# A gate row moved to the second issuing queue, x tiles copied in halves, two groups of loads planned earlier and a new scheduler seed, in a kernel for gated attention and feed-forward

## The chip, the cores and the metric

The kernel runs on one core of a Trainium2 chip. The metric is the time of one execution in device microseconds (us), and lower is better. An execution is timed several times; its state is "fast" where no core shows a lowered clock and the time is within 1.5% of the best of the same kernel.

The core has five engines that run their own instruction streams: PE (the tensor engine), ACT (ScalarE), DVE (VectorE), POOL (GpSimd) and SP (SyncE), which in this kernel only issues transfers. Engines wait for one another by semaphores.

## The reference, cut to what matters

```python
# x: [1, 2048, 512] bf16; 32 heads of 16; 4 segments of 512 tokens; F = 1792
g = sigmoid((x * gate_w).sum(-1, keepdims=True))
# a: per segment, masked softmax attention plus a read of a memory M, z
for s in range(4):
    a_dot = softmax(q_s @ k_s.T * 0.25 + mask) @ v_s
    a_mem = (phi(q_s) @ M) / (phi(q_s) @ z + 1e-6)     # phi(t) = t + 1 if t > 0 else exp(t)
    o_s = sigmoid(beta) * a_mem + (1 - sigmoid(beta)) * a_dot
    M, z = M + phi(k_s).T @ v_s, z + phi(k_s).sum()
a = concat(o) @ wo
b = (relu(x @ W_gate) * (x @ W_up)) @ W_down
out = g * a + (1 - g) * b
```

`gate_w` is one row of 512 values (1 KB). All 2048 tokens are multiplied by it, so the kernel keeps it copied to all 128 partitions, in `gwb`.

## The kernel before: the parts that the change and the argument touch

The program is not written in its final order. A list scheduler in it is given operations, each with what it reads and writes, a priority and, for some, an earliest planned time (`after`, in ns of a plan). A seeded random jitter breaks near-ties. The result is a fixed program for each engine. So an edit of a planned time or of the seed can change the order of everything.

```python
sc = Sched(seed=197)
...
def load(eng, names, dst, src, nbytes, occ=460.0):          # one transfer, on ACT's or SP's ring
    (lact if eng == "act" else lsp).append(dma(eng, lambda e, ...: e.dma_start(dst, src), ...))
x0 = A_x[0, 0:512, :].rearrange("(i p) d -> p i d", p=128)
for n, src in enumerate((A_wq[0:16, 0:32], gate_w[0:32].partition_broadcast(16),
                         W_g[0:16, 0:32], W_u[0:16, 0:32], W_d[0:16, 0:32])):
    load("act", [f"touch{n}"], V.touch[0:16, n, :], src, 1024)   # 1 KB reads whose data nobody uses
for i in range(4):
    load("sp", [f"hT{i}"], V.hT[:, i, :], x0[:, i, :], 1 << 17)  # the four x tiles of segment 0
for nm, w, src in (("wq", V.wq, A_wq), ("wk", V.wk, A_wk), ("wv", V.wv, A_wv)):
    for kt in range(KT):
        if nm == "wk" and kt == 0:
            load("sp", ["gwb"], V.gwb[:], gate_w.partition_broadcast(128), 1 << 17)
        load("sp", [f"{nm}{kt}"], w[:, kt, :], src[kt * 128:(kt + 1) * 128, :], 1 << 17)
... # then beta, W_gate and W_up in eight pieces each half, x of segment 1, wo, and at last:
load("sp", ["wd"], V.wd[:], W_d.rearrange("(f p) n -> p f n", p=128), NF * 128 * 1024)
...
for c in range(2, NSEG):                                    # x of segments 2 and 3 ("chunks")
    load_x(c)                                               # four transposing transfers
    for t in lsp[-KT:]:
        t.after = 30000.0 + 10000.0 * (c - 2)
sc.queue(3, lsp)
```

Segment 0 of x comes as plain tiles `hT`, which PE transposes by a product with the identity; DVE and ACT copy the result from the accumulation banks (`psL`) to `xT`. The first q projection needs `xT`. Around these stand matmuls on constants (`warm`) that keep PE busy.

```python
xps, xcs = [warm(5, 512, 0, 3)], []
for n, (i, k0, k1, bank, eng) in enumerate(((0, 0, 4, 0, "dve"), (1, 0, 4, 1, "act"),
        (2, 0, 4, 2, "dve"), (3, 0, 2, 3, "dve"), (3, 2, 4, 0, "act"))):
    ...                                                     # PE: transpose; then the copy:
    if eng == "dve": ... e.tensor_copy(d, s_)
    else:            ... e.activation(d, s_, ACT.Copy)
xps.append(warm(5, 128, 1, 1))
```

Five names recur. `ek` and its transposed copy `phik` are phi(k) of a segment, which PE needs to update the memory. `gscr` is a 2 KB scratch in DRAM through which the gate values `gexp` are turned round to `gexpT`. `vsh` is a shifted copy of v. `osb` receives the x tiles of later segments for the gate. `wd` is the 1792 KB of W_down.

The softmax here doesn't subtract the row's maximum and nothing guards it: scores larger than these inputs give would overflow.

## Time and profile before

| | before |
|---|---|
| median of the first three runs | 272.04 us (271.92 to 272.37) |
| the run that was profiled, and its span | 272.65 us, 270.5 us |
| first q matmul, first k matmul | 5.92 us, 9.37 us |
| `wd` issued, landed | 25.78 us, 35.42 us |
| chunk 2 of x: first issue, last landing | 36.83 us, 44.60 us |
| first matmul that needs chunk 2 | 44.84 us, after a wait of 1.79 us |

All times in it but the first row are from the start of the span. The prediction shows the issue queue and PE's waits. Two more views belong beside them. The first is the head of the page's chain of waits, followed back from the last instruction: shares of the span by the engine that held up the end. The second is the table of stretches from 36 to 56 us and from 56 to 100 us: stretch, its length, then busy time and instructions of PE, of PE's weight loads, of DVE, ACT and POOL, the granted clock, the DMA share and the GB/s.

```profile
PE 87%; SPq 7%; DMA 3%; DVE 1%; issue 1%; ACT 0%
```

```profile
36.00:56.00 20.00, 17.98 (x272) 8.23 (x272) 15.00 (x29) 15.46 (x12) 9.03 (x17) 1.00 0.57 88
56.00:100.00 44.00, 43.99 (x523) 19.86 (x524) 37.55 (x74) 37.40 (x34) 22.91 (x47) 1.00 0.22 44
```

Issues and transfers hold a tenth of the chain, and PE lacks 2.02 us between 36 and 56 us and next to nothing (0.01 us) from 56 to 100 us.

### The profile page before, as it was taken

What the parts mean: (1) busy time and instruction counts of PE and PEld (TensorE: products, weight loads), DVE (VectorE), ACT (ScalarE), POOL (GpSimd) and SP (SyncE); (2) the same over time, 40 slices, a digit from 0 to 9 for tenths busy, and PEclk for the clock granted to TensorE, in tenths of its full rate; (3) what the DMA queues carried; (4) which work ended last, traced back from release to release, by engine and by line L of the source; (5) the groups of instructions that cost most, each with busy time, mean ns of one, the idle gap of its engine ahead of it and who ended that gap; (6) DMA issues with size and microseconds to landing.
All of it is one profiled execution on the core that took longest, in us unless ns stands there. A gap on an engine that the chain in (4) does not pass through costs nothing.

```text
span 270.5 us, 6903 instructions
## 1 busy us (share of the span) xinstructions
PE 264.3 (98%) x2908; PEld 117.7 (43%) x2908; DVE 187.5 (69%) x360; ACT 185.2 (68%) x160; POOL 110.4 (41%) x227
## 2 busy tenths in 40 slices
PE   7999997999999999999999999999999999999996
PEld 3344443444454435444444444444444444444444
DVE  5798786888988687787867849766666444597200
ACT  3577886787898875677787867786766567772122
POOL 5024545574248424762376225622282228220000
PEclk9999999999999999999999999999999999999999
DMA  6899994610033232210012110100111100000011
GB/s 166 233 380 197 337 130 62 101 40 22 19 63 43 61 79 61 61 21 2 21 41 61 39 41 23 41 2 0 23 41 39 41 22 19 2 0 2 0 39 41
DMA packets 35150, 17.70 MB, mean 65 GB/s; under 512 B 23984, under 2 KB 35120, under 8 KB 35120
## 3 DMA queue, kind: packets, MB, share of 16 engines
q1 hardware_dynamic: 34960, 17.26, 27.9%
q8 instruction: 23, 0.38, 0.6%
q14 instruction: 7, 0.06, 0.1%
q10 hardware_dynamic: 160, 0.01, 0.0%
HBM read 9.88 MB, written 2.11 MB: 44 GB/s over the span
## 4 chain that ended last, share of the span: by engine, by line
PE 87%; SPq 7%; DMA 3%; DVE 1%; issue 1%; ACT 0%
PE psA L879 35%; PE psA L918 18%; PE psL L747 8%; PE psA L643 7%; PE psA L911 5%; PE psA L806 5%; PE psA L641 4%; SPq L497 4%; SPq L475 2%; DMA osb<-in_A_x_dram 2%; DMA wk<-in_A_wk_dram 1%; PE psA L717 1%; PE psA L814 1%; SPq L603 1%; PE psA L688 1%
## 5 line engine op out<-in xcount | busy, mean ns | idle before, releaser
L755 ACT ACTIVATE E<-psL 128x2048 bf16<-128x2048 f32 x72 | 135.0, 1876 | 39.2 <-PE psL L747 37.6
L773 POOL TENSOR_SCALAR_AFFINE_SELECT E<-E 128x256 bf16<-128x256 bf16 x128 | 52.6, 434 | 106.9 <-ACT E L755 99.8
L879 PE MATMUL psA<-xT,wu 128*128 128x512 bf16 x224 | 59.8, 380 | 0.0
L879 PE MATMUL psA<-xT,wg 128*128 128x512 bf16 x224 | 59.4, 380 | 0.2 <-DVE hT L890 0.2
L918 PE MATMUL psA<-wd,hT 128*128 128x512 bf16 (+2 forms) x238 | 54.1, 367 | 0.0
L791 POOL TENSOR_SCALAR_AFFINE_SELECT E<-E 64x512 bf16<-64x512 bf16 (+1 forms) x64 | 41.1, 671 | 18.9 <-ACT E L755 10.7
L890 DVE TENSOR_TENSOR hT<-psA,rl 128x512 bf16<-128x512 f32 x56 | 38.0, 680 | 15.0 <-PE psA L879 13.9
L825 DVE STREAM_TRANSPOSE Tn<-psA 128x512 f32<-128x512 f32 x32 | 21.3, 696 | 18.2 <-PE psA L814 18.0
L887 ACT ACTIVATE rl<-psA 128x512 bf16<-128x512 f32 x32 | 19.1, 596 | 18.1 <-PE psA L879 17.6
L918 PEld LDWEIGHTS psA<-wd,hT 128*128 128x128 bf16 x238 | 21.3, 98 | 23.2 <-issue 1.7
L879 PEld LDWEIGHTS psA<-xT,wg 128*128 128x128 bf16 x224 | 20.4, 98 | 24.5 <-issue 1.9
L879 PEld LDWEIGHTS psA<-xT,wu 128*128 128x128 bf16 x224 | 20.2, 98 | 24.1 <-issue 2.1
L747 PE MATMUL psL<-qT,kp 32*128 32x64 bf16 (+3 forms) x768 | 28.7, 245 | 0.0
L747 PEld LDWEIGHTS psL<-qT,kp 32*128 32x128 bf16 x768 | 9.9, 92 | 30.6 <-issue 20.8
L660 DVE TENSOR_SCALAR kp<-kT,pm 128x512 bf16<-128x512 bf16 (+1 forms) x32 | 12.8, 420 | 10.6 <-PE psL L747 10.2
L888 DVE TENSOR_SCALAR rl<-psA 128x512 bf16<-128x512 f32 x24 | 16.5, 686 | 3.8 <-PE psA L879 3.2
L643 PE MATMUL psA<-xT,wq 128*128 128x512 bf16 x64 | 16.2, 380 | 2.2 <-DMA xT<-in_A_x_dram 1.8
L928 ACT ACTIVATE osb<-psA,omg 128x512 bf16<-128x512 f32 (+2 forms) x10 | 6.4, 645 | 15.7 <-PE psA L911 13.2
L806 PE MATMUL psA<-E,vaug 128*17 128x192 bf16 (+3 forms) x512 | 16.8, 273 | 0.1
L643 PE MATMUL psA<-xT,wk 128*128 128x512 bf16 x64 | 16.5, 380 | 0.4 <-DMA wk<-in_A_wk_dram 0.4
L911 PE MATMUL psA<-wo,oT 128*128 128x512 bf16 (+2 forms) x68 | 16.5, 367 | 0.0
L641 PE MATMUL psA<-wv,xT 128*128 128x512 bf16 x64 | 15.7, 380 | 0.0
(78 smaller groups left out, 235.6 us busy)
## 6 DMA issues: line engine op xcount, KB each, us to landing
out_dram<-osb SPq DMA_DIRECT2D x15, 128.0 KB, 1.7
wg<-in_B_W_gate_dram SPq DMA_DIRECT2D x8, 224.0 KB, 5.3
wu<-in_B_W_up_dram SPq DMA_DIRECT2D x8, 224.0 KB, 5.6
wd<-in_B_W_down_dram SPq DMA_DIRECT2D x1, 1792.0 KB, 9.6
osb<-in_A_x_dram SPq DMA_DIRECT2D x12, 128.0 KB, 2.1
vsh<-vaug SPq DMA_DIRECT2D x4, 136.0 KB, 2.5
hT<-in_A_x_dram SPq DMA_DIRECT2D x4, 128.0 KB, 2.4
wq<-in_A_wq_dram SPq DMA_DIRECT2D x4, 128.0 KB, 2.8
```

The lines of the kernel that those rows point to most:

```text
L641: ins = e.matmul(A(ep)[:, :], lhsT=V.xT[:, kt, tok + col * 128:tok + (col + 1) * 128], rhs=w[:, kt, :], start=(kt == 0), stop=(kt == KT - 1))
L643: ins = e.matmul(A(ep)[:, :], lhsT=w[:, kt, col * 128:(col + 1) * 128], rhs=V.xT[:, kt, tok:tok + 512], start=(kt == 0), stop=(kt == KT - 1))
L747: ins = q.matmul(PL[:, jj, o:o + w], lhsT=kap(jj), rhs=V.qT[32 * jj:32 * jj + 32, qs, q0:q0 + w], start=True, stop=True, tile_position=(32 ...
L755: acts.append(act(lambda a, eout=eout: a.activation(eout, PL[:, :, :] if slot is None else PL[:, :, :].rearrange("q h (g c) -> q h g c", g ...
L773: pools.append(pool(lambda g, ap=ap: g.affine_select(out=ap, in_=ap, compare_op=ALU.is_ge, fill=0.0, base=64, pattern=[[0, 4], [1, 64]], c ...
L791: pools.append(pool(lambda e, ap=ap, base=base: e.affine_select(out=ap, in_=ap, compare_op=ALU.is_ge, fill=0.0, base=base, pattern=[[0, 8] ...
L806: ins = q.matmul(A(eps[p])[32 * jj:32 * jj + 17, 512 - w:512], lhsT=V.vaug[:, s % 2, j, p, 4 * G + jj, :], rhs=V.E[:, e, jj, o:o + w], sta ...
L825: ds.append(dve(lambda e, p=p, ep=eps[p]: e.transpose(V.Tn[:, p, :], A(ep)[:, :]), t_dve(512), writes=[f"Tn{p}"], name=f"tr{s}_{G}_{p}", e ...
L879: ins = e.matmul(A(ep)[:, :], lhsT=w[:, kt, f * 128:(f + 1) * 128], rhs=V.xT[:, kt, c * 512:(c + 1) * 512], start=(kt == 0), stop=(kt == K ...
L890: evs.append(dve(lambda e, ep=eu, r=r, hs=hs: e.tensor_tensor(V.hT[:, hs, :], A(ep)[:, :], V.rl[:, r, :], ALU.mult), t_dve(512), reads=[f" ...
L911: ins = e.matmul(A(ep)[:, 0:c1 - c0], lhsT=V.oT[:, o0 + G, i * 128:(i + 1) * 128], rhs=V.wo[:, G, c0:c1], start=st_ and G == 0, stop=sp_ a ...
L918: ins = e.matmul(A(ep)[:, 0:c1 - c0], lhsT=V.hT[:, slots[f], i * 128:(i + 1) * 128], rhs=V.wd[:, f, c0:c1], start=st_ and f == f0, stop=sp ...
```

## The change

The intent is to take a transfer out of the crowded queue of SP, to let DVE and ACT share the copies of x more evenly, and to have chunks 2 and 3 of x earlier. The seed is new as well, and three touches are planned later. The core of the diff:

```diff
-    sc = Sched(seed=197)
+    sc = Sched(seed=140)
...
-    for n, src in enumerate((A_wq[0:16, 0:32], gate_w[0:32]..., W_g[0:16, 0:32], ...)):
+    def touch(n, src):
         load("act", [f"touch{n}"], V.touch[0:16, n, :], src, 1024)
+    touch(0, A_wq[0:16, 0:32])
+    load("act", ["gwb"], V.gwb[:], gate_w.partition_broadcast(128), 1 << 17)
...
-            if nm == "wk" and kt == 0:
-                load("sp", ["gwb"], V.gwb[:], gate_w.partition_broadcast(128), 1 << 17)
...
+    for n, w in enumerate((W_g, W_u, W_d)):
+        touch(n + 1, w[0:16, 0:32])
+        lact[-1].after = 6500.0
...
-            t.after = 30000.0 + 10000.0 * (c - 2)
+            t.after = 26000.0 + 12000.0 * (c - 2)
...
-    ... (2, 0, 4, 2, "dve"), (3, 0, 2, 3, "dve"), (3, 2, 4, 0, "act")
+    ... (2, 0, 2, 2, "dve"), (2, 2, 4, 0, "act"), (3, 0, 2, 3, "dve"), (3, 2, 4, 1, "act")
...
-                gq["dve"][-1].after = 6000.0
+                gq["dve"][-1].after = 6300.0
```

Cut from it are the names of the sixth copied piece, the pieces that the first three q projections wait for, the bank of the second `warm`, and the touch of `gate_w`, which is dropped because the gate row itself now stands in its place.

More of the change, by code (lines that the diff above doesn't have):

```diff
@@ L412, in plan @@
         ("braw", [128, 32], BF16), ("eb", [128, 32], F32), ("romgh", [128, 32], F32), ("epsv", [128, 32], F32),
-        ("gexp", [128, NT], F32), ("omg", [128, NT], F32), ("gexpT", [128, NT * 4], F32), ("c2g", [128, 2, 4, 32], F32), ("gwb", [128, 512], BF16), ("touch", [128, 5, 32], BF16), ("gl", [128, NT], F32),
+        ("gexp", [128, NT], F32), ("omg", [128, NT], F32), ("gexpT", [128, NT * 4], F32), ("c2g", [128, 2, 4, 32], F32), ("gwb", [128, 512], BF16), ("touch", [128, 4, 32], BF16), ("gl", [128, NT], F32),
         ("rden", [128, 32], F32), ("rdg", [128, 32], F32), ("rdm", [128, 128], F32), ("pm8", [128, 8], F32), ("pm", [128, 2], F32), ("pmb", [128, 64], BF16), ("ident", [128, 128], BF16),
@@ L469, in xt @@
     def xt(c):
-        return [f"xT{c}_{kt}" for kt in range(KT)] if c else [f"xT0_{i}" for i in range(5)]
+        return [f"xT{c}_{kt}" for kt in range(KT)] if c else [f"xT0_{i}" for i in range(6)]
     lact, lsp = [], []
@@ L476, in program @@
     x0 = A_x[0, 0:512, :].rearrange("(i p) d -> p i d", p=128)
-    for n, src in enumerate((A_wq[0:16, 0:32], gate_w[0:32].partition_broadcast(16), W_g[0:16, 0:32], W_u[0:16, 0:32], W_d[0:16, 0:32])):
+    def touch(n, src):
         load("act", [f"touch{n}"], V.touch[0:16, n, :], src, 1024)
+    touch(0, A_wq[0:16, 0:32])
+    load("act", ["gwb"], V.gwb[:], gate_w.partition_broadcast(128), 1 << 17)
     for i in range(4):
@@ L506, in program @@
     sc.queue(0, lsp)
+    lact = []
+    for n, w in enumerate((W_g, W_u, W_d)):
+        touch(n + 1, w[0:16, 0:32])
+        lact[-1].after = 6500.0
+    sc.queue(0, lact)
     lsp = []
@@ L549, in program @@
     xps, xcs = [warm(5, 512, 0, 3)], []
-    for n, (i, k0, k1, bank, eng) in enumerate(((0, 0, 4, 0, "dve"), (1, 0, 4, 1, "act"), (2, 0, 4, 2, "dve"), (3, 0, 2, 3, "dve"), (3, 2, 4, 0, "act"))):
+    for n, (i, k0, k1, bank, eng) in enumerate(((0, 0, 4, 0, "dve"), (1, 0, 4, 1, "act"), (2, 0, 2, 2, "dve"), (2, 2, 4, 0, "act"), (3, 0, 2, 3, "dve"), (3, 2, 4, 1, "act"))):
         def fx(e, i=i, k0=k0, k1=k1, bank=bank):
@@ L562, in program @@
             xcs.append(act(lambda e, d=dst, s_=srcp: e.activation(d, s_, ACT.Copy), t_act(w), reads=[f"bankL{bank}"], writes=[f"xT0_{n}"], name=f"xc{n}"))
-    xps.append(warm(5, 128, 1, 1))
+    xps.append(warm(5, 128, 1, 2))
     sc.queue(0, xps)
@@ L644, in fn @@
                     return ins
-                pes.append(pe(fn, mm(512, step), reads=[f"{wname}{kt}" for kt in range(k0, k0 + step)] + (xt(s) if not early or k0 > 1 else xt(s)[:4]), name=f"{name}{s}_{col}", ep=ep, role="w2" if k0 else "w"))
+                pes.append(pe(fn, mm(512, step), reads=[f"{wname}{kt}" for kt in range(k0, k0 + step)] + (xt(s) if not early or k0 > 1 else [x for x in xt(s) if x not in ("xT0_3", "xT0_5")]), name=f"{name}{s}_{col}", ep=ep, role="w2" if k0 else "w"))
             return ep
```

## The prediction

> **What bounds the kernel now.** I read the page's busy table first, then the timeline of the tensor engine (PE), the timeline of the DMA issues on SyncE (SPq), and last the timeline of VectorE (DVE) and ScalarE (ACT) in the first 13 us. First the page, then PE's timeline cut to the lines before which it stood idle.
>
> ```profile
> PE 264.3 (98%) x2908; PEld 117.7 (43%) x2908; DVE 187.5 (69%) x360; ACT 185.2 (68%) x160; POOL 110.4 (41%) x227
> ```
>
> ```profile
> 0.84 2.29 PE L545 MATMUL psL<-const-bfloat16-1.0 128*128 128x512 bf16 x5 [0.84 <-PEq L1020]
> ...
> 4.31 0.76 PE L553 MATMUL psL<-ident,hT 128*128 128x128 bf16 x8 [0.17 <-DMA hT<-in_A_x_dram]
> ...
> 5.92 3.61 PE L643 MATMUL psA<-xT,wq 128*128 128x512 bf16 x16 [0.37 <-DVE xT L560]
> ...
> 10.32 2.32 PE L643 MATMUL psA<-xT,wk 128*128 128x512 bf16 x10 [0.35 <-DMA wk<-in_A_wk_dram]
> ...
> 44.84 1.02 PE L643 MATMUL psA<-xT,wq 128*128 128x512 bf16 x4 [1.79 <-DMA xT<-in_A_x_dram]
> ...
> 55.97 0.60 PE L879 MATMUL psA<-xT,wg 128*128 128x512 bf16 x2 [0.23 <-DVE hT L890]
> ```
>
> Columns are start, length, engine and line; in brackets is the idle time ahead and what ended it. PE is the bound from about 56 us on: the table of stretches gives it 43.99 of 44.00 us from 56 to 100, and no less than 49.88 of 50 in each stretch from 100 to 250. What is left to win lies before 56 us: 0.37 before the first q projection, 0.35 for a tile of wk, 1.79 for chunk 2 of x, 0.23 behind DVE. That is 2.74 us; with the start of the x transposes nearly the whole of what any change to loads can gain, 1.0% of 272.04.
>
> The 1.79 us is the large one, and what sets it is seen in the issue queue of SyncE:
>
> ```profile
> 2.66 1.85 SPq L475 DMA_DIRECT2D wq<-in_A_wq_dram  x4
> 4.56 0.43 SPq L475 DMA_DIRECT2D gwb<-in_gate_w_dram  x1
> 5.03 1.86 SPq L475 DMA_DIRECT2D wk<-in_A_wk_dram  x4
> ...
> 25.78 0.53 SPq L475 DMA_DIRECT2D wd<-in_B_W_down_dram  x1
> 26.35 2.44 SPq L601 DMA_DIRECT2D gscr<-gexp  x1
> 28.89 7.90 SPq L667 DMA_TRANSPOSE phik<-ek  x4
> 36.83 5.17 SPq L497 DMA_TRANSPOSE xT<-in_A_x_dram  x4
> 42.10 2.90 SPq L603 DMA_DIRECT2D gexpT<-gscr  x4
> 45.04 5.03 SPq L497 DMA_TRANSPOSE xT<-in_A_x_dram  x4
> 50.11 0.58 SPq L591 DMA_DIRECT2D osb<-in_A_x_dram  x1
> ```
>
> Each row begins within 0.13 us of the end of the row above it in that timeline, from 0.80 to 50.7 us. The queue has no idle time at all, so a load comes when the queue reaches it, whatever its planned time. Chunk 2 is the last group before 42.0 us, lands at 44.6 us and PE waits until 44.84. The page's chain of waits agrees: from 34.73 to 54.65 us it runs over SPq and DMA rows, not over PE. So two bounds stand one after the other: SyncE's queue to about 55 us, then PE.
>
> Why the queue is late also shows. The 2 KB write of gscr holds the queue for 2.44 us where a plain issue takes 0.43, and the four phik transposes take 7.90 us where four xT ones take 5.17. Both stand behind wd, 1792 KB, issued at 25.78 and landed 9.6 us later by the table of DMA issues. I read this as back-pressure of the transfers ahead.
>
> **What the Trainium skill says.** "DMA: Bandwidth & Descriptors", section "Issuing engines are not separate DMA queues": DMAs from several engines run on the same 16 DMA engines and interleave; a second issuer saves only the sequencer's issue time. The trace gives that time, 0.43 us for gwb; no run yet shows the interleaving of a large load. The same page, "Queues, rings and completion order": each DMA engine takes descriptors of one ring in ring order; that fits gscr and phik landing after wd (37.2 to 39.5 against 35.4 us). "TensorE: Matmul & The Clock Gate", "Back-to-back issue gap": N/2.4 + 2.5 ns, for 512 columns 216 ns; here the first q matmuls start at 5.916 and 6.131, 215 ns apart. So PE's stream itself cannot be shortened by this change. "ScalarE: Activation LUTs", "What ACT_TABLE_LOAD costs": about 1283 ns; here one load took 1.28 us, at 3.13, right after the last of the five touch issues.
>
> **The change part by part.**
>
> Gate row. Leaves SPq: one issue of 0.43 us and its gap, 5.03 − 4.56 = 0.47 us. Everything behind it on SPq may come 0.47 us earlier. There is a second effect. Landings in the trace: the last wq at 6.79, gwb at 8.40, the first wk at 8.80, the next two 0.33 us apart. gwb's slot is thus 1.61 us, where its neighbours of equal size take about 0.33 us: some 1.28 us of transfers are delayed. On the ACT ring, issued near 1.24 us, it competes with the x tiles instead. Its 128 KB costs them at least 0.33 us; if the slow slot comes along, up to 1.3 us. wk loses it: its last tile would land about 1.3 + 0.47 us earlier than 10.18, so the 0.35 us wait goes. The gate multiplications on DVE (4 of 0.69, overlapping, about 2.5 us), which waited for gwb till 8.43 us, move into DVE's idle stretch of 2.66 us before that, and DVE reaches the q and k copies some 2 us less loaded. That is beside PE, and worth no time there by itself.
>
> Touches. ACT issued five, 0.80 to 3.10 us, then the table load until 4.42 us, and only then its copy of x tile 1 at 4.43. Now it issues two (to about 1.7 us), loads the table until about 3.0, and can copy tile 1 when PE is done with it, near 4.1: about 0.3 us earlier, beside DVE's work. The other three touches, 3 x 0.47 = 1.4 us, fall after 6.5 us, where ACT has 2.77 us idle (5.50 to 8.27). Free.
>
> Copies in halves. Before, DVE: 0.69 (tile 0), 0.69 (tile 2), 0.41 (half of 3), ending at 5.77; ACT: 0.60 and 0.38. After, DVE: 0.69 + 0.41 + 0.41, ACT: 0.60 + 0.38 + 0.38. DVE saves 0.28 us on the path to the first q matmul, 5.92 to about 5.6. Against it stands the 0.33 us or more by which gwb delays the x tiles: I book 0.0 for the start, between −0.3 and +0.5. It matters little: it is swallowed by the wait at 44.84 us, since PE cannot pass that point before chunk 2 lands.
>
> Chunks 2 and 3 forward. Planned times 30 and 40 us become 26 and 38. But the queue was full before and chunk 2 stood behind the phik transposes, which have higher priority in this program. An earlier planned time removes no wait in a full queue; it pays only if the new order puts chunk 2 ahead of phik or gexpT. The seed changes too, so the order may change. If chunk 2 went first entirely, it would gain up to four slots of 1.3 us and the wait would vanish; phik would then be later, and PE's memory update needs it (it met phik just as it landed, at 38.0 us).
>
> Sum, read at the point where PE waits for chunk 2 (44.84 us): 0.47 less issue, an estimated 0.5 less back-pressure (of the 1.28 us of delay, part is taken back by faster landings), 0.2 for the chance of a better order (about one in eight of the 1.79): −1.2 us, 270.8 us. The waits at 5.92 and 10.32 are not added, being swallowed by it.
>
> **The rivals.** (1) The order improves and the wait for x disappears. Then all the early waits count: 0.35 + 1.79 + 0.23 + about 0.3 = 2.7, so 269.4. For it speaks that the move is aimed at this wait; against it the gapless queue and phik's priority. (2) A new wait replaces the old: phik lands late and the memory update stalls, or gexpT or the first gate tile (osb landed at 54.59, DVE waited 1.16 us) gets later against a faster PE. Speaks for it that both were met with no slack; it costs 0.5 to 2 us, 271.5 to 272.8. (3) The transfer was hidden anyway: the relief on SPq is eaten behind wd, which is bound by bytes, and the gain is under 0.4: 271.7. (4) gwb's slow slot, moved to the front, delays x and wq by a microsecond: wq had 0.4 to 1.1 us of slack (wq tile 1 landed at 6.14, used at 6.56). It delays the start, mostly swallowed; at worst 272.5.
>
> **Range and chances.** I weigh the main line at half with 270.5 to 271.3, rival 1 at a quarter, the others together at a quarter. That gives 270.8 with 269.1 to 272.6 as the range. Faster by 2% needs under 266.6, 5.4 us; all waits before 56 us sum to 2.74, so only a shorter stream would do it: 3%. Slower by 2% needs 5.4 us of new waits: 2%.
>
> **What would show it.** Right: the gwb issue gone from SPq and wk at about 4.6 us; no wait for wk near 10 us; first q matmul within 0.4 us of 5.92; SPq still gapless to about 50 us; chunk 2 landing 0.5 to 1.5 us before 44.6 with PE still waiting for it; PE from 56 us on as busy as before. Wrong: chunk 2 ahead of phik in the queue and no wait for it (faster than said), a new wait of over 0.5 us for phik, gexpT or osb between 38 and 60 us, or the first q matmul after 6.5 us (slower).

## The result, and the profile after

| | before | after |
|---|---|---|
| median of six runs | 272.03 us (271.92 to 272.37) | 271.55 us (270.28 to 272.08) |
| ratio of means, 95% interval | | 0.9973 (0.9951 to 0.9995) |
| profiled run, span | 272.65, 270.5 us | 271.08, 268.9 us |
| x tiles landed | 2.98, not recorded, 4.27, 4.63 | 2.93, 4.29, 5.26, 5.61 |
| first q, first k matmul | 5.92, 9.37 | 6.74, 10.78 |
| `wd` issued, landed | 25.78, 35.42 | 24.21, 33.43 |
| chunk 2: first issue, last landing | 36.83, 44.60 | 34.09, 41.31 |
| first matmul that needs chunk 2 | 44.84 | 43.70 |

A ratio here is the mean time of one kernel's fast runs over that of the other's fast runs of the same rounds, so it is not quite the ratio of the medians. The changed kernel is faster by 0.27%, a small gain whose interval just excludes 1. The two profiled runs differ by 1.57 us, the medians by 0.48: so one look at each, the trace of a single profiled run, overstates the change, since it can fall anywhere in its kernel's spread. That of before is above all six of its timed runs.

The page's busy table and the head of its chain of waits, after:

```profile
PE 259.8 (97%) x2870; PEld 118.8 (44%) x2908; DVE 187.2 (70%) x359; ACT 186.1 (69%) x162; POOL 112.5 (42%) x227
```

```profile
PE 93%; DVE 2%; issue 2%; DMA 1%; SPq 0%; ACT 0%; DVEq 0%
```

The busy time of PE can't be set against that of before: this trace has 2870 of 2908 matmul records, as the count shows. The chain can. The issue queue is gone from it. Next, SP's issues after, those that answer to the rows that the prediction shows of before:

```profile
4.66 1.86 SPq L475 DMA_DIRECT2D wk<-in_A_wk_dram  x4
...
24.21 0.50 SPq L475 DMA_DIRECT2D wd<-in_B_W_down_dram  x1
24.75 2.39 SPq L606 DMA_DIRECT2D gscr<-gexp  x1
27.24 6.81 SPq L672 DMA_TRANSPOSE phik<-ek  x4
34.09 5.74 SPq L497 DMA_TRANSPOSE xT<-in_A_x_dram  x4
```

The order is that of before: chunk 2 behind `phik`, `phik` behind `wd`. The whole has moved forward, `wk` by 0.37 us, `wd` by 1.57, chunk 2 by 2.74. Now PE's timeline after, cut to the stretches of interest:

```profile
4.34 0.61 PE L558 MATMUL psL<-ident,hT 128*128 128x128 bf16 x4 [0.76 <-DMA hT<-in_A_x_dram]
5.31 1.04 PE L558 MATMUL psL<-ident,hT 128*128 128x128 bf16 x8 [0.36 <-DMA hT<-in_A_x_dram]
...
6.74 4.20 PE L648 MATMUL psA<-xT,wq 128*128 128x512 bf16 x16
10.78 2.75 PE L648 MATMUL psA<-xT,wk 128*128 128x512 bf16 x11
...
43.70 0.59 PE L648 MATMUL psA<-xT,wq 128*128 128x512 bf16 x2
```

Two things stand in it. The waits for `wk` and for chunk 2 are gone: the row at 43.70 has no bracket. And the start has become worse. PE now waits 0.76 and 0.36 us for x tiles, and the first 16 q matmuls take 4.20 us where before they took 3.61. The single records show why: the first three gaps from start to start are 419, 426 and 384 ns, the others 215 to 216, and before all are 215 to 216. "TensorE: Matmul & The Clock Gate", section "Wait — 56ns, not 53.3ns?" of the Trainium skill, gives start to start of 426.7 ns for 512 columns and 106.7 ns for 128 while the array is cold, and 215.7 and 55.6 warm. The trace agrees: the last eight x transposes after are 106 to 107 ns apart but for one gap of 82, before mostly 56 to 66. PE ran at half rate at its start, for longer than before.

The last stretch that changed, in the columns explained above:

```profile
36.00:56.00 20.00, 19.74 (x280) 9.36 (x280) 17.61 (x33) 16.73 (x15) 9.69 (x18) 1.00 0.36 75
```

PE is busy 1.76 us longer in it than before, at least, as some records are missing. So the account by the two traces is: the first k matmul 1.41 us later (0.82 before the first q matmul, 0.59 in the q matmuls at half rate); the first matmul on chunk 2, 1.14 us earlier; the end 1.6 us earlier. A loss of 1.4 us at the start has been more than made up by 44 us. Which part of the change did that was the question for the experiments. Part of the two starts' difference is scatter: D1 below runs the same program as the changed kernel up to the issue of `wd`, and in its look the first k matmul came 0.91 us later still.

### The profile page after: what moved, and what is told of

Same layout as the page of the kernel before. It is cut to its first block, busy times and chain, and to the rows that moved or that the text cites. A ratio compares the mean times of both kernels' runs of the same rounds, so it can differ in the third digit from the quotient of the medians.

```text
span 268.9 us, 6868 instructions
## 1 busy us (share of the span) xinstructions
PE 259.8 (97%) x2870; PEld 118.8 (44%) x2908; DVE 187.2 (70%) x359; ACT 186.1 (69%) x162; POOL 112.5 (42%) x227
## 4 chain that ended last, share of the span: by engine, by line
PE 93%; DVE 2%; issue 2%; DMA 1%; SPq 0%; ACT 0%; DVEq 0%
PE psA L884 36%; PE psA L923 17%; PE psA L648 11%; PE psL L752 9%; PE psA L811 5%; PE psA L916 5%; PE psA L646 5%; PE psA L819 1%; DMA hT<-in_A_x_dram 1%; PE psA L722 1%; PE psA L693 1%; PE psA L709 0%; DVE Tn L830 0%; PE psL L558 0%; SPq L475 0%
## 5 line engine op out<-in xcount | busy, mean ns | idle before, releaser
L884 PE MATMUL psA<-xT,wg 128*128 128x512 bf16 x218 | 57.9, 379 | 0.8 <-issue 0.8
L884 PE MATMUL psA<-xT,wu 128*128 128x512 bf16 x211 | 57.1, 380 | 1.6 <-issue 1.0
L923 PE MATMUL psA<-wd,hT 128*128 128x512 bf16 (+2 forms) x227 | 51.8, 366 | 1.2 <-issue 1.0
L796 POOL TENSOR_SCALAR_AFFINE_SELECT E<-E 64x512 bf16<-64x512 bf16 (+1 forms) x64 | 42.5, 689 | 22.7 <-ACT E L760 13.0
L893 DVE TENSOR_SCALAR rl<-psA 128x512 bf16<-128x512 f32 x25 | 17.2, 690 | 5.4 <-PE psA L884 4.5
L933 ACT ACTIVATE osb<-psA,omg 128x512 bf16<-128x512 f32 (+2 forms) x13 | 8.5, 654 | 16.6 <-PE psA L916 10.5
L648 PE MATMUL psA<-xT,wq 128*128 128x512 bf16 x64 | 17.1, 391 | 0.0
L648 PE MATMUL psA<-xT,wk 128*128 128x512 bf16 x59 | 15.4, 379 | 0.5 <-issue 0.3
L665 DVE TENSOR_SCALAR kp<-kT,pm 128x512 bf16<-128x512 bf16 (+1 forms) x32 | 11.6, 379 | 4.9 <-PE psL L752 4.8
L646 PE MATMUL psA<-wv,xT 128*128 128x512 bf16 x62 | 14.6, 380 | 0.3 <-issue 0.3
```

Of the source, the lines that this page charges most:

```text
L646: ins = e.matmul(A(ep)[:, :], lhsT=V.xT[:, kt, tok + col * 128:tok + (col + 1) * 128], rhs=w[:, kt, :], start=(kt == 0), stop=(kt == KT - 1))
L648: ins = e.matmul(A(ep)[:, :], lhsT=w[:, kt, col * 128:(col + 1) * 128], rhs=V.xT[:, kt, tok:tok + 512], start=(kt == 0), stop=(kt == KT - 1))
L796: pools.append(pool(lambda e, ap=ap, base=base: e.affine_select(out=ap, in_=ap, compare_op=ALU.is_ge, fill=0.0, base=base, pattern=[[0, 8] ...
L884: ins = e.matmul(A(ep)[:, :], lhsT=w[:, kt, f * 128:(f + 1) * 128], rhs=V.xT[:, kt, c * 512:(c + 1) * 512], start=(kt == 0), stop=(kt == K ...
L923: ins = e.matmul(A(ep)[:, 0:c1 - c0], lhsT=V.hT[:, slots[f], i * 128:(i + 1) * 128], rhs=V.wd[:, f, c0:c1], start=st_ and f == f0, stop=sp ...
```

## The experiments

**The theories.** T says that the gate row's move did it: it frees a slot of SP's queue, the queue was the bound, chunk 2 comes earlier, and the worse start is the price. Its rival O (order) says that the order which the new seed and planned times give carries the gain, and that the gate row alone brings none. A third question goes with both: whether the start's loss counts at all, or whether the queue, the later bound, takes back whatever the start gains. Where an expectation speaks of a rival, it is the other view of these, or the one that it spells out.

**How edits were isolated.** Changing anything that the scheduler sees re-plans the program. So most kernels below keep the order: the plan is made as in the parent kernel, and then one item is moved in one engine's finished program. `cut` takes an item out of an engine's program by name, `put_after` puts it behind a named item. Where the gate row is put later than its parent has it (B1, B2, D4) it gets its own semaphore, so that no later transfer has to wait for it. Only the two kernels marked "re-planned" differ in the order of other work. All outputs are right. All twelve kernels ran in five rounds (six runs each) beside the kernel before on the same chip (four chips in all). "Slow matmuls" is my count, from the traces, of starts more than 300 ns apart among the first 16 q matmuls (in B2 a gap of 1.01 us, a wait for `wq`, is left out). "Chunk 2" is its last landing; the last column is the first matmul that needs it.

| kernel | ratio to before (95%) | median us | first q | slow matmuls | chunk 2 | needed |
|---|---|---|---|---|---|---|
| before | 1 | 272.03 | 5.92 | 0 | 44.60 | 44.84 |
| after | 0.9973 (0.9951–0.9995) | 271.55 | 6.74 | 3 | 41.31 | 43.70 |
| A1 before, gate row on ACT | 1.0039 (1.0014–1.0065) | 273.38 | 7.55 | 10 | 42.04 | 46.10 |
| A2 before, touches late | 1.0006 (0.9988–1.0024) | 272.16 | 5.94 | 0 | 44.44 | 44.69 |
| B1 after, gate row on SP | 0.9962 (0.9934–0.9990) | 271.33 | 5.59 | 2 | 42.96 | 43.60 |
| B2 after, gate row late on ACT | 0.9948 (0.9923–0.9973) | 270.84 | 6.05 | 1 | 41.32 | 43.53 |
| B3 after, filler matmuls | 0.9951 (0.9925–0.9977) | 271.01 | 7.37 | 0 | 43.03 | 43.75 |
| C1 after, gate row spread by PE | 0.9959 (0.9939–0.9980) | 270.99 | 5.99 | 0 | 42.88 | 43.28 |
| C3 after, planned times 30/40 (re-planned) | 1.0009 (0.9990–1.0029) | 272.25 | 6.94 | 9 | 42.28 | 45.42 |
| C4 after, seed 197 (re-planned) | 1.0048 (1.0029–1.0067) | 273.22 | 6.92 | 0 | 42.82 | 43.06 |
| D1 after, `wd` late | 0.9968 (0.9938–0.9999) | 271.68 | 7.01 | 6 | 40.42 | 44.61 |
| D2 = C1 + `wd` late | 0.9931 (0.9893–0.9969) | 269.69 | 5.77 | 0 | 38.41 | 42.16 |
| D3 before, `wd` late | 0.9995 (0.9954–1.0036) | 272.17 | 5.98 | 0 | 40.03 | 42.97 |
| D4 = B1 + `wd` late | 0.9932 (0.9916–0.9948) | 270.02 | 5.94 | 0 | 39.02 | 42.81 |

Read the column "first q" first. The six kernels that send the gate row early on ACT's ring as 128 copies (after, A1, B3, C3, C4, D1) begin at 6.74 to 7.55 us, the eight others at 5.59 to 6.05. No other column is so clearly divided.

The slow matmuls can be checked against the clock records of the traces. In C3 these records, which lie in the packed trace, have the granted clock at 0.5 for 3.41 us, from 7.05 to 10.46, where its nine slow matmuls lie; this alone gives that run its mean of 0.994. In the other looks with slow ones the first record, at 1.0, begins where these end: at 7.92 us in the changed kernel, 11.83 in A1, 9.49 in D1, 6.40 in B1, 6.34 in B2. The time before the first record counts as full clock, so a mean of 1.00 does not exclude slow matmuls at the start.

A landing is less firm. B3 issues the same transfers in the same order as the changed kernel, and its chunk 2 landed 1.7 us later. Two looks at transfers in the order of before gave 44.60 and 44.44. A difference of landings under some 1.7 us between two looks therefore proves nothing.

### A1: the gate row's move alone, in the order of before

```diff
+ put_after(sc, "act", "ldtouch0", cut(sc, "sp", "ldgwb"))     # order of before kept
```

> The kernel before with one edit: the gate row load is issued on ACT behind the first touch, in the order of every engine that the kernel before has. Theory T (the gate row costs the x tiles at the start, and frees the weights and SyncE's queue behind it): the first q matmul comes at 6.5 to 6.9 us instead of 5.92, with some matmuls 430 ns apart instead of 216; the last tile of x chunk 2 lands 1.5 to 3 us before 44.6; PE's wait for it falls from 1.79 to under 0.5 us; time 270.5 to 271.3. Rival R (the wait for chunk 2 went because of the new order of instructions, not because of the gate row): chunk 2 lands at most 0.7 us earlier, PE still waits over 1 us for it; time 271.6 to 272.2.

Measured: 0.39% slower, 273.38 us, outside both expected ranges. The landing moved as T says, 2.56 us earlier, beyond the scatter, and PE's wait for chunk 2 is gone. The time did not follow, and the first q matmul, at 7.55, is later than T's 6.9. PE's start in A1:

```profile
4.76 0.61 PE L592 MATMUL psL<-ident,hT 128*128 128x128 bf16 x4 [1.20 <-DMA hT<-in_A_x_dram]
...
7.55 5.71 PE L682 MATMUL psA<-xT,wq 128*128 128x512 bf16 x16 [0.24 <-DVE xT L599]
```

PE waits 1.20 us for the second x tile, and the 16 q matmuls take 5.71 us. To see how far a delay travels, I compare the starts of the 72 softmax exponentials on ACT, which have the same order in both kernels. Against before, A1 lags 3.10 us at the first, 3.12 at the ninth, 1.28 at the eleventh, 0.80 from the seventeenth on. The lag falls at the point where before waits for chunk 2 and A1 does not. It does not fall to zero. (The profiled run was A1's slowest, 274.17, with ten slow matmuls; the median is less.) The gate row's move frees the queue and delays the start, and by itself it costs.

### A2: the touches late, in the order of before

```diff
+ for n in (4, 3, 2):
+     put_after(sc, "act", "xc4", cut(sc, "act", f"ldtouch{n}"))
```

> The kernel before with only the touches of W_gate, W_up and W_down moved behind ACT's second x copy, all else in its own order. Theory: the touches cost and save nothing that can be seen: first q matmul within 0.2 us of 5.92, PE waits 1 to 2.3 us for chunk 2, time 271.8 to 272.4. Rival (touches in front of the loads slow or speed the DMA engines): chunk 2 lands over 2 us from 44.6, or the time moves by over 0.5 us.

Measured: 1.0006, the same. PE's wait for chunk 2 stayed, at 1.9 us. The touches cost nothing and save nothing where they stand. This was tried in the order of before only; moving them early in the changed order would have reused a semaphore too soon, and was not run.

### B1: the gate row back on SP, in the changed order

```diff
+ put_after(sc, "sp", "ldwq3", cut(sc, "act", "ldgwb"))        # order of after kept
```

> The changed kernel with one part undone: the gate row is issued on SyncE ahead of wk again, all else in the changed kernel's order. Theory T: first q matmul at 5.5 to 5.9 us, no matmuls at 430 ns; chunk 2 lands 1.5 us or more later than 41.3 us; PE waits 0.5 to 2 us for it or for wk; time 270.6 to 271.4. Rival R: chunk 2 lands within 0.7 us of 41.3, no wait for it; the start is 1.2 us earlier and all of it reaches the end: time 270.0 to 270.4.

Measured: 271.33 us, ratio 0.9962, with an interval that overlaps that of the changed kernel almost wholly. The time, the first q matmul (5.59) and the landing of chunk 2 (1.65 us later) are what was expected under T. But PE did not wait for chunk 2 or `wk`, and two slow matmuls stayed. And undoing the main item of the change leaves the time where it was, so the gate row's move is not what carries the gain. The exponentials show how. Against the changed kernel, B1 leads by 1.10 us at the first, by 0.92 at the seventh, by 0.09 at the ninth, and lags by 0.47 from the thirteenth to the end. The lead is lost at two places, one on PE and one on DVE:

```profile
37.85 0.66 PE L734 MATMUL psA<-vaug,phik 128*128 128x136 bf16 x8 [0.76 <-DMA phik<-ek]
```

```profile
46.61 0.21 DVE L879 TENSOR_TENSOR rdg<-rden,gexpT 128x32 f32<-128x32 f32 x1 [2.12 <-DMA gexpT<-gscr]
```

PE, being early, stands before `phik`, and DVE before `gexpT`. Both are transfers that SP issues behind `wd`. In the look at the changed kernel neither wait exists: its PE and DVE get there later, and its queue was earlier. Its last `gexpT` read landed at 43.11 us, 1.40 before its use at 44.51. B1's was issued at 43.19 and landed at 46.59; the 3.4 us on the way, against 1.7 in the changed kernel (C1: 3.1), are most of DVE's wait, and why they are so long is not known.

### C1: the gate row read once and spread by PE, in the changed order

```diff
+ # ACT reads 1 KB into partition 0 of gwb; PE: ones[1,128].T @ gwb[0:1,:]; ACT copies the bank to gwb
+ g[1].fns = {"act": lambda e: e.dma_start(gwb[0:1, :], gate_w.rearrange("(o n) -> o n", o=1))}
```

> The changed kernel, but only the single 1 KB gate row is read (same place on ACT) and PE spreads it to 128 partitions with one matmul on ones, ACT copies it out; the order of all else is the changed kernel's. Theory T2 (reading the row 128 times, 128 KB, is what delays the x tiles): first q matmul at 5.4 to 5.8 us, first k matmul by 9.4 us instead of 10.78, chunk 2 lands at 40 to 43 us, PE waits at most 0.4 us in all between 38 and 56 us; time 269.6 to 270.4. Rival (SyncE's queue takes back what the start gains, as it did with the gate row on SyncE): start as above, but waits of 0.8 us or more for phik, chunk 2 or a gate tile; time 270.8 to 271.5.

This takes the row off both queues as a burden: no 128 KB of transfers, no place on SP. Measured: the start was mended (first q at 5.99 us, no slow matmul), and the time was 270.99 us, ratio 0.9959, in the rival's range and not in T2's. The lead of 1.32 us at the first exponential shrinks to 0.45 at the ninth and turns into a lag of 0.15 from the thirteenth on. The rival was right again, and at the same two places:

```profile
37.49 0.67 PE L741 MATMUL psA<-vaug,phik 128*128 128x136 bf16 x8 [0.68 <-DMA phik<-ek]
```

```profile
46.29 0.21 DVE L886 TENSOR_TENSOR rdg<-rden,gexpT 128x32 f32<-128x32 f32 x1 [2.15 <-DMA gexpT<-gscr]
```

So in these two looks a microsecond won at the start came to nothing: the queue, the next bound, took it back. In them the queue was also about 1.1 to 1.3 us later at `wd` (25.54 and 25.32 us) than in the look at the changed kernel (24.21), although C1 has no gate row on SP either. B3 with 25.30 shows the same, and D1, the changed kernel's program up to there, reached that place at 25.47. That is scatter of the queue, not an effect of the edits. With a queue as early as in the look at the changed kernel, its spare time of 1.40 us at `gexpT` and 2.39 us at chunk 2 (landed 41.31, used 43.70) would have let most of such a lead through, by my estimate. So how much is taken back differs from run to run. The medians of B1, B2 and C1 are 0.2 to 0.7 us below that of the changed kernel, with intervals that overlap.

### B2 and B3: two other ways to spare the start

```diff
+ put_after(sc, "act", "xc1", cut(sc, "act", "ldgwb"))         # B2: the row behind ACT's first copy of x
+ put_after(sc, "pe", "xt0", fill(8)); put_after(sc, "pe", "xt1", fill(12))   # B3: constant matmuls
```

> The changed kernel with the gate row issued on ACT after its first x copy (near 4.7 us), so that it is neither ahead of the x tiles nor in SyncE's queue. Theory T: first q matmul at 5.5 to 5.9 us and no matmuls at 430 ns, so 1.2 us earlier than in the changed kernel; chunk 2 lands at 41.3 to 42.5 us and PE waits under 0.5 us for it; time 270.0 to 270.6. Rival: the gate row keeps its slow slot wherever it stands, wk lands late and DVE, which now waits for the gate row until about 8.4 us, delays PE by about as much as the start gained: time 271 to 271.6.

> The changed kernel with 20 small matmuls on constants put where PE waits for x tiles 1 and 2 (8 after tile 0, 12 after tile 1), nothing else changed. If the q matmuls 430 ns apart come from PE's idle time at the start: all q matmuls are 216 ns apart, the first q matmul is up to 0.3 us earlier, and the time is 0.5 to 0.9 us below the changed kernel's, 270.6 to 271.0, with a spread under 1 us instead of 1.8. Rival: the slow matmuls have another cause, or the start is not on the path: slow ones stay, or time within 0.2 us of 271.5.

B2 issued the row at 4.19 us instead of 1.24. The x tiles came in time (first q 6.05), but now the last tile of `wq` landed at 8.87 and PE waited 0.6 us for it. At the exponentials the lead over the changed kernel is only 0.34, then 0.17 us. The median of 270.84 is 0.7 below that of the changed kernel; the intervals overlap. It lies between the ranges of the two views; that `wq` and `wk` land late is what the rival said.

B3 took PE's idle time away: 20 matmuls on constants stand where it had waited for x tiles. All slow matmuls vanished, and the x transposes behind the fillers are 55 to 56 ns apart. The fillers ran past the landing of the tiles, so the first q matmul came at 7.37. Both effects cancel, the lag being 0.05 us. Its time against the changed kernel is unclear. The expected end of the slow matmuls came; an earlier first q matmul and a spread under 1 us (it was 1.43) did not. That idle PE alone makes the slow matmuls is not settled: C4 below waited as long for x tiles and had none.

### C3 and C4: the order taken apart

```diff
-            t.after = 26000.0 + 12000.0 * (c - 2)      # C3, re-planned
+            t.after = 30000.0 + 10000.0 * (c - 2)
-    sc = Sched(seed=140)                                # C4, re-planned
+    sc = Sched(seed=197)
```

> The changed kernel with only the planned times of the loads of chunks 2 and 3 put back to 30 and 40 us, planned anew by its own scheduler. The issue order on SyncE up to the end of chunk 2 is the same as in the changed kernel, so chunk 2 lands within 2 us of 41.3 (the scatter that two runs with the same issue order showed) and PE does not wait for it. Theory O (the planned times act only through the order of instructions that the planner then finds, which the seed was chosen for): more waits of PE after 56 us, 272.3 to 274. Rival (the planned time of chunk 2 matters by itself): a wait of over 1 us for chunk 2 near 43 us. Rival (neither matters): within 0.4 us of 271.5.

> The changed kernel with only the seed put back to 197, planned anew. Theory O (a good part of the gain is the seed's order): 272.3 to 274, slower than the kernel before. Rival (the loads and copies are the gain, the seed is noise): 271.2 to 271.9.

Each is the changed kernel but for one line. C4 measured 1.0048, with an interval (1.0029 to 1.0067) wholly above that of the changed kernel: with the old seed the change is a loss, as O expected. C3 measured 1.0009 and shows no gain over before, but its interval (0.9990 to 1.0029) still touches that of the changed kernel (0.9951 to 0.9995), and its 272.25 us is just under O's range. In both, chunk 2 landed as early as with the others (42.28 and 42.82 us). What is new are waits on PE, in the table of waits by engine and line (microseconds in total, times, longest), first C3, then C4:

```profile
PE psL L752 <- ACT E L760: 0.5, 1, 0.5
PE psA L811 <- ACT kp L667: 0.4, 1, 0.4
```

```profile
PE psL L752 <- ACT E L760: 1.7, 2, 1.0
PE psA L648 <- DMA xT<-in_A_x_dram: 0.4, 1, 0.4
```

The waits for ACT lie at 75 and 128 us in C3, at 65 and 89 us in C4, well after chunk 2 and its queue. In C4's look the account closes: its first k matmul is 0.41 us ahead of the changed kernel's, the two waits for ACT (0.77 and 0.97) and the one for chunk 2 (0.39) sum to 2.1 us, and its last matmul ends 1.68 us later. Its ratio less that of the changed kernel, 1.0048 − 0.9973, is 0.75% or 2.0 us. So O is right as to the seed: with 197 in the place of 140 the gain is lost to waits in the order. As to the planned times it is not settled: of the 1.9 us by which C3's look ends later, 1.3 are there at the first k matmul already, with nine slow q matmuls. B1 agrees with O from the other side: it is the change without its gate row's move, and has the whole gain. The kernel before with seed 140 alone, which would say what the order gives without any other edit, was not run.

### D1 to D4: the large load out of the queue's way

If the queue ahead of `phik` is the bound that eats every gain, moving what stands in it must make gains at the start arrive at the end. `wd` is 1792 KB, is issued at about 25 us and first used at 89.2 us before and 85.7 after. All four kernels keep their parent's order and issue it behind the first reads of `gexpT`:

```diff
+ put_after(sc, "sp", "grd0", cut(sc, "sp", "ldwd"))
```

> The changed kernel with the one large load of wd (1792 KB) issued on SyncE behind the first gexpT reads instead of ahead of gscr, phik and chunk 2; all else in its order. Theory Q (wd ahead in the ring is what makes phik, chunk 2 and the gate tile late, and PE of the changed kernel does not wait for any of them because it starts late): gscr issues in under 1 us, chunk 2 lands at 35 to 39 us, PE's stream is not shifted: time within 0.4 us of 271.5. Rival (the queue is late by its own issue times, not by wd): chunk 2 lands at 40 us or later.

> The changed kernel with the gate row spread by PE and wd issued late, both edits together. Theory Q: now the start's gain of 1.2 to 1.3 us, which the wait for phik and one after 52 us took back with the first edit alone, reaches the end: no wait of over 0.3 us between 30 and 56 us, time 269.6 to 270.4, faster than both kernels. Rival (another wait takes it back again, for example DVE or the banks of PSUM): 270.8 or more.

> The kernel before with one edit: wd issued behind the first gexpT reads. Theory Q: chunk 2 lands at 36 to 40 us, the wait of 1.79 us for it and the one of 0.23 us near 56 us are gone: time 269.6 to 270.5. Rival (the queue is late by its own issue times): chunk 2 lands at 42 us or later and the time stays within 0.6 us of 272.04.

> The changed kernel with the gate row back on SyncE ahead of wk (as in the second run) and wd issued late (as in the three runs before): the changed order without the move of the gate row, and with the queue relieved. If the move to ACT costs the start 1.1 us or more and its gain lies in the queue alone: first k matmul near 9.4 us, no wait of over 0.4 us between 30 and 56 us, profile 0.9 to 1.5 us below that of the changed kernel, time 270.0 to 270.9. Rival (the gate row on SyncE comes too late for DVE, which holds PE): waits near 50 to 56 us as in the second run, time 271.2 or more.

D1 is the changed kernel with this one move: 271.68 us, as without it and as Theory Q expected. `gscr` took 0.44 us as expected too, but chunk 2 landed at 40.42 us, where the rival had it, not at 35 to 39. That does not speak for the rival's cause, the queue's own issue times: here SP stood idle for 2.0 us before `phik`, until DVE had finished `ek` at 27.89. In all four D kernels the first `phik` transpose starts within 0.1 us of the end of `ek`, so there the queue is no longer what holds it. Its start happened to be slow, first q at 7.01 and six slow matmuls. Against the changed kernel its exponentials lag by 0.91 us at the first and by 0.91 at the last: nothing is won in between, since the changed kernel has no wait left on the queue, and nothing is taken back.

D4 is B1, and D2 is C1, with the same move. There the lead of the start reaches the end: D4 leads the changed kernel by 0.89 us from the third exponential to the last, D2 by 1.55. B1 and C1 without the move had ended at lags of 0.47 and 0.15. SP's issues in D4:

```profile
25.63 0.45 SPq L648 DMA_DIRECT2D gscr<-gexp  x1
26.17 5.18 SPq L714 DMA_TRANSPOSE phik<-ek  x4
31.40 6.23 SPq L539 DMA_TRANSPOSE xT<-in_A_x_dram  x4
37.73 1.95 SPq L650 DMA_DIRECT2D gexpT<-gscr  x4
39.72 0.43 SPq L517 DMA_DIRECT2D wd<-in_B_W_down_dram  x1
```

The 2 KB write of `gscr` takes 0.45 us here and 2.39 in the changed kernel, and four `phik` transposes take 5.18 against 6.81. What the prediction read as back-pressure of `wd` (an issue held up because the transfers ahead of it are not done) is shown by this move. It goes where `wd` goes: the four transposes of chunk 3 behind it now take 8.99 us, where they took 5.89 in the changed kernel, but nobody waits for them. `wd` landed at 49.1 us, 36 us before its first use. PE's stretch from 36 to 56 us is now full:

```profile
36.00:56.00 20.00, 20.00 (x282) 9.43 (x275) 18.09 (x34) 16.50 (x15) 9.33 (x17) 1.00 0.77 158
```

D4 measured 0.9932 of before, with an interval (0.9916 to 0.9948) wholly below that of the change (0.9951 to 0.9995), and its six runs lie between 269.79 and 270.46. It beats both kernels. D2 has the better look and four runs below 269.8, but two at 271.8 and 272.0, so its mean is no better. Why those two were slow is not known; no trace of one was taken.

D3, before with the move, missed its expectation. The look is nearly as expected: the wait for chunk 2 (landed 40.03) is gone, one of 0.32 us for DVE near 54 us is left, and from the eleventh exponential on it leads before by 1.8 us. But the six times run from 270.45 to 273.88, with a median of 272.17. The likely reason is that the start scatters from run to run, and a wait later on had absorbed that; the looks with the most slow matmuls (A1 ten, C3 nine, D1 six) are each the slowest of their kernel's six runs. D3's slowest run has a mean clock of 0.994, as C3's look has; the next two, 273.03 and 272.64, read 1.00. No trace of a slow run of D3 exists, so this stays open.

## Why the prediction was right or wrong

The time was right as a range: 271.55 lies within 269.1 to 272.6, and the predicted 270.8 was 0.75 us too low. Of the signs that the prediction set for itself, wrong ones came on both sides: the first q matmul after 6.5 us ("slower"), and no wait for chunk 2 ("faster than said"), though without its condition, a new order in the queue. So the fit of the number is in part luck.

- **The two bounds in a row** were right. Before, both chunk 2 and `phik` came when the queue reached them; D2 and D4 show that a gain at the start reaches the end once the queue is relieved, and B1 and C1 that it can be taken back before.
- **The slot of 0.47 us on SP** was right: `wk` went 0.37 us forward and the first x transpose of chunk 1 0.47 (17.58 to 17.11). The wait for `wk` ended, as said, but not as worked out: its last tile landed 0.53 us earlier (10.18 to 9.65), not 1.3 + 0.47, and PE also came later.
- **Earlier planned times don't move chunk 2 in a full queue**: right. It stayed behind `phik`, and with the old times (C3) it landed at 42.28 us, within the scatter. The touches being free was right too (A2).
- **ACT's copy 0.3 us earlier** was wrong. ACT was indeed ready at 3.00, but x tile 1 landed at 4.29 and the copy began at 4.98, not 4.43. The freed engine only waited for data.
- **The step that failed is "I book 0.0 for the start, between −0.3 and +0.5".** Measured: +0.82 us at the first q matmul and +1.41 at the first k. The delay, "up to 1.3 us" for the x tiles, had been named here and in rival 4 ("delays x and wq by a microsecond") and then booked at 0.33; the tiles came about 1.0 us late. The half rate of PE behind it was not foreseen at all.
- **"With PE still waiting for it" failed with it.** The start was to be swallowed by the wait for chunk 2. But chunk 2 came 3.28 us earlier in the look, not the 0.5 to 1.5 predicted, and PE came later. In that look no wait was left to swallow the start, and a loss goes through where none is, as D1 shows for its own 0.91 us. Where the queue ran later (B1, C1), waits for `phik` and `gexpT` took back a start that was better by as much.
- **The term "an estimated 0.5 less back-pressure" was too small** in that look: of the 2.74 us by which chunk 2's issue moved forward, 1.57 were won before `wd` and 1.09 in the `phik` transposes. A part of it is scatter: 1.26 us at the place of `wd` by D1, 1.7 us at the landing by B3.
- **The order got 0.2 us and was the larger thing.** The prediction looked for a better order in SP's queue only, where nothing changed. C4 shows that it lay later, in waits of PE for ACT (1.7 us) that a less lucky order has. So the sum came near the truth with two terms off in opposite directions, a loss at the start and more relief of the queue than was booked, and with the order on which both depended.

Not tried: the copies in halves alone, since they change what the scheduler sees. Their saving of 0.28 us on DVE is neither shown nor refuted.

## What to carry to other kernels

See whether the issue queue has any idle time before moving a load: in a gapless queue a large transfer that nobody needs yet is the thing to move back, behind the small ones that somebody waits for. A gain ahead of a bound can be invisible until the bound itself moves, so test the two edits together as well as apart. And where a scheduler with a seed makes the program, keep the order fixed while testing an edit, or the order's own gain or loss (here 0.75% for C4 against the changed kernel) will be put down to the edit.

## What the Trainium skill lacked or had wrong

- "DMA: Bandwidth & Descriptors", section "Issuing engines are not separate DMA queues", says of a second issuing engine that it only saves the sequencer's time, "usually small relative to the DMA itself". Here it was on the path: SP issued without a gap from 0.80 to 50.7 us, and one issue less brought `wk` forward by 0.37 us.
- The same page has no number for one row read 128 times over. The 1 KB gate row spread to 128 partitions took a slot of 1.61 us in the landings of before (1.2 to 1.7 in the four other looks with it on SP) where plain tiles of equal size took 0.33, and on the other ring the last x tile landed at 5.61 to 6.07 us instead of 4.43 to 5.00 with the row on SP; read once and spread by PE (C1, D2) it landed at 5.01 and 4.54.
- The same page does not say that a large transfer ahead holds up the issue of small ones on its ring: a 2 KB issue behind 1792 KB took 2.39 to 2.92 us, without it 0.44 to 0.58.
- "TensorE: Matmul & The Clock Gate" has the ramp's cost at under 1% of a typical span and advises against fitting to a count of cold matmuls. The figures of start to start agree (107 and 426 ns), and so does the bound: ten slow matmuls in A1, some 0.21 us each, are 0.8% of its span. But the kernels compared here differ by less, so in a tuned kernel it is of the size of what is sought. Here the profile's mean clock hid it: the column reads 1.00 from 0 to 20 us in the changed kernel, whose clock records begin at 7.92 us only, and 0.51 from 7.0 to 10.4 us in C3.
- "ScalarE: Activation LUTs", section "What ACT_TABLE_LOAD costs", adds a drain of about 1380 ns to the load of 1283 for every switch to a different set. The load took 1.28 us here, and before, the copy behind it began at 4.43 us, 0.01 after its end at 4.42; no drain was seen behind it. It was the one load of the program, and the page's figure is for a switch, which no run here has.
